# Local attention scores: one 128-key matmul, or two of 64 keys in 32x64 tiles of TensorE

## The chip, the cores and the metric

The kernel runs on one core of one Trainium2 chip. The core has five engines that run their own instruction streams and meet through semaphores: TensorE (PE in the profile; its weight loads are listed as PEld), VectorE (DVE), ScalarE (ACT), GpSimd (POOL) and SyncE (SP). TensorE multiplies a stationary operand, loaded first by a LDWEIGHTS instruction, with a moving operand that streams through, and writes sums to PSUM, which has eight banks of 2 KB on each of 128 partitions. A matmul that contracts over fewer than 128 rows, or gives fewer than 128 output partitions, occupies only a part of the array, a tile; "32x128" means 32 rows of contraction by 128 output partitions.

The metric is the device time of one execution in microseconds, the median of several runs. The profile is one execution, recorded instruction by instruction; its span runs from the first to the last instruction.

## What is computed

```python
# q_l, k_l, v_l: (8 batches, 8 heads, 512 tokens, 64); q_g, k_g, v_g: the same with 32 global tokens
s_g  = scale * q_g @ concat(k_g, k_l).T          # global queries see every key
out_g = softmax(s_g) @ concat(v_g, v_l)
s_ll = where(abs(pos_q - pos_k) <= 32, scale * q_l @ k_l.T, -1e9)   # local: a band of 65 keys
s_lg = scale * q_l @ k_g.T
out_l = softmax(concat(s_lg, s_ll)) @ concat(v_g, v_l)
x = concat(out_g, out_l, axis=2)                 # to (8 * 544 tokens, 512)
h = x @ w_in                                     # 512 -> 2048
out = (h / (1 + exp(-1.702 * h))) @ w_out        # 2048 -> 512
```

Inputs and outputs are float32; the products take bf16 operands and sum in float32.

## The kernel before

**Tiling of the attention.** The 64 pairs of batch and head are worked in 16 quads of four heads. In a quad, head j lies on the partitions 32j to 32j+31. A head has 64 features; 32 of them lie on the strip's partitions, and each 32-bit cell holds two bf16 features, so that a feature pair is picked by the index e (0 or 1) with a step of two elements. The tile `k` holds a quad's keys, `q` its queries, both turned by VectorE (L271, L275). Queries are stored as t, r (16 t by 32 r), and some rows of global queries are copied to the ends of the same tile (L285), so that one matmul gives the scores of a block of local queries and of the global queries.

**The scores, `S` (L300).** Keys are cut in four chunks c of 128. Two chunks make a round, so that a quad has two rounds. For chunk c only a window of queries can lie in the band: `WIN[c]` gives 10 or 12 values of r, and with 20 or 19 values of t these are 200 or 228 columns. For each chunk, `S` issues for e = 0 and 1, and for the four heads j, one matmul with lhsT = 32 rows by 128 keys and rhs = 32 rows by 200 or 228 columns (L314). It writes all 128 partitions of head j's bank, `ps[j]`: four heads, four banks. A call is thus a burst of 2 x 2 x 4 = 16 matmuls with their 16 weight loads. The first call of all is cut in two parts by query columns, since half of the queries are turned first.

**What follows a burst.** `X` (L347) applies the exponential on ScalarE, from the banks to the tile `e` in SBUF; `M` (L354) multiplies the band mask on VectorE. `gg` and `K` (L333) give the scores of the global keys in 32x32 tiles, `ekU` (L400) and `U` (L426) the products with values and the row sums, in 32x32 and 128x32 tiles; `Gm` (L444) those of the global queries.

**The feed-forward part.** `h_mm` (L495) multiplies x with `w_in`, 64 matmuls of 128x128 by 512 columns for a batch; `h_act` (L502, L503) applies the activation; `o_mm` (L520) multiplies with `w_out`, again 64 matmuls of 512 columns, in four groups of 16.

**The order of the work.** It is written out by hand: a Tile program whose scheduler is off (`manual_schedule`), so that each engine executes in the order of the Python code. In the steady part, `phase_o(i)` (L728) runs the output matmuls of batch i in four groups of 16, and puts the attention of batch i+1 between them: one call of `S` before each group, some of them followed by `gg`, `ekUs`, `U` and `Gm`. Then the 64 matmuls of `h_mm` for batch i+1 follow. DMAs for later batches are issued on GpSimd's queue (`load`, `load_v`), the outputs on SyncE's.

Of the kernel before, what the change touches and what calls it, by code (L numbers as in the profile page):

```python
# [20 lines left out]
def kernel(  # L21
# [12 lines left out]
    nc = tc.nc  # L34
# [211 lines left out]
    def bank(pair, j):  # L246
        return pair[j // 2][:, j % 2, :]

    class Quad:
# [50 lines left out]
        def S(self, rnd, split=False, added=False, part=None):  # L300
            if not added:
                self.bk[rnd] = self.spt(rnd)
            ps = self.bk[rnd] if split else [bank(self.bk[rnd], j) for j in range(4)]
            for c in (2 * rnd, 2 * rnd + 1):
                off = (0, 200, 0, 228)[c]
                r0, nr = WIN[c]
                t0, t1 = ((0, 20), (4, 23), (1, 20), (4, 24))[c]
                lo, hi = ((t0, t1) if part is None else (12, t1) if part else (t0, 12))
                off += (lo - t0) * nr
                n = (hi - lo) * nr  # L310
                for e in range(2):
                    for j in range(4):
                        p = slice(32 * j, 32 * j + 32)
                        nc.tensor.matmul(  # L314
                            ps[j][:, off : off + n],
                            lhsT=self.k[p, 128 * c : 128 * c + 128, e],
                            rhs=self.q[p, lo:hi, r0 : r0 + nr, e],
                            start=(e == 0 and not added), stop=(e == 1), skip_group_check=True,
                        )
            if not part:  # L320
                self.E[rnd] = att.tile([128, 4, RW + 32], BF16, name="e%d" % rnd)
            if split:
                self.gk(ps[2][:, RW : RW + 32], self.qg)
            self.ps = self.bk[rnd]
# [200 lines left out]
    def o_out(i, tci, op):  # L525
        ob = moe.tile([128, d_model], F32, name="ob", bufs=6)
        last = i == B and tci == B // 4 - 1
        for lo, hi in ((0, 320), (320, 512)) if last else ((0, 512),):
            if last:
                op = pbank("op")  # L530
                for fc in range(FC):
                    nc.tensor.matmul(op[:, lo:hi], lhsT=gTs[i][:, fc, tci * 128 : tci * 128 + 128],  # L532
                                     rhs=w_out_sb[:, fc, lo:hi], start=(fc == 0), stop=(fc == FC - 1))
            nc.scalar.activation(ob[:, lo:hi], op[:, lo:hi], AF.Copy, scale=0.5)  # L534
            for j in range(4):
                eng = nc.scalar if last and j % 2 else nc.sync
                if i < B:
                    rows = out[i * S + Sg : (i + 1) * S, :].rearrange("(r t) m -> t r m", t=16)[4 * tci + j]
                else:
                    r = (4 * tci + j) * S  # L540
                    rows = out[r : r + Sg, :]
                eng.dma_start(out=rows[:, lo:hi], in_=ob[32 * j : 32 * j + 32, lo:hi])  # L542
# [8 lines left out]
    a, c = Quad(0), Quad(1)  # L551
# [99 lines left out]
    a, c = nq[1]  # L651
# [48 lines left out]
    a, c = nq[2]  # L700
# [128 lines left out]
```

## Time and profile before

| | before |
|---|---|
| time, median of 3 runs | 307.6 us (307.58 to 308.48) |
| span of the profiled execution | 305.3 us |
| the profiled execution's own time | the page gives none apart from its span; the span is 2.3 us below the median |
| TensorE busy | 298.7 us, 98% |
| VectorE, ScalarE, GpSimd busy | 211.2, 169.3, 55.7 us |
| output matmuls, L520 | 528, 122.0 us busy |
| input matmuls of 512 columns, L495 | 496 (and 64 of 256 columns), 108.9 us busy |
| score matmuls, L314 | 528, 21.2 us busy, mean 280 ns each |
| weight loads of L314 | 528, mean 95 ns each |
| TensorE's granted clock | 1.000 |

How to read it. A matmul's duration is the time from its start until its results are in PSUM; matmuls are pipelined, so that a stream of 512-column matmuls that last 380 ns each starts one every 216 ns. Busy time counts overlapping matmuls once. The share of the chain that ended last tells what the end of the kernel waited for; idle time of an engine that is not in that chain costs nothing. In views of a short stretch, the number after x counts the instructions that touch the stretch, those that started before it among them.

### The profile page before, as it was taken

To read this page: it belongs to the slowest core of one execution; us is meant where nothing else is said; L and a number is where in the kernel's file an instruction comes from. 1 tells how busy PE (TensorE), PEld (TensorE's weight loads), DVE (VectorE), ACT (ScalarE), POOL (GpSimd) and SP (SyncE) were. 2 spreads that over 40 slices of the span, in tenths; PEclk is the share of its full clock that TensorE was granted. 3 is DMA by queue.
4 is the path that set the end of the run, shared out by engine and by line. 5 is a ranking of instruction groups with operands and counts; after the bars stand their busy time and mean duration, and the time that the engine had idled before them with its cause. 6 is when DMAs were issued, how large, how long until landed. Compare 5 with 4: busy or idle time off the path is not lost.

```text
span 305.3 us, 7862 instructions
## 1 busy us (share of the span) xinstructions
PE 298.7 (98%) x3265; PEld 148.5 (49%) x3265; DVE 211.2 (69%) x445; ACT 169.3 (55%) x282; POOL 55.7 (18%) x89
## 2 busy tenths in 40 slices
PE   7999999999999999999999999999999999999995
PEld 6454445445454455445454455445454454446653
DVE  6678858978868876777767876787677855573320
ACT  4738484585556655575457654665456661673421
POOL 8732755530050002300050002100000000000000
PEclk9999999999999999999999999999999999999999
DMA  7999999999399023941299024901130021101122
GB/s 191 178 206 207 197 180 230 211 170 131 82 112 191 10 56 84 151 97 37 54 122 170 4 56 89 101 0 48 44 86 2 2 66 48 46 0 36 36 63 75
DMA packets 56436, 29.52 MB, mean 97 GB/s; under 512 B 43088, under 2 KB 46288, under 8 KB 56400
## 3 DMA queue, kind: packets, MB, share of 16 engines
q0 software_dynamic: 46000, 16.98, 49.9%
q1 hardware_dynamic: 9920, 11.39, 14.3%
q10 hardware_dynamic: 480, 0.66, 0.7%
q8 instruction: 25, 0.41, 0.6%
q14 instruction: 11, 0.09, 0.1%
HBM read 35.13 MB, written 8.91 MB: 144 GB/s over the span
## 4 chain that ended last, share of the span: by engine, by line
PE 80%; DMA 15%; DVE 2%; POOL 1%; issue 1%; ACT 0%; ACTq 0%; DVEq 0%; POOLq 0%
PE op L520 34%; PE hp L495 33%; DMA rk<-in_k_l_dram 10%; PE s L314 5%; PE ov L426 4%; DMA rq<-in_q_l_dram 3%; DMA w_in_sb<-in_moe_w_in_dram 2%; PE ov L400 2%; DVE xL L459 1%; PE op L532 1%; PE s L444 1%; PE s L333 1%; ACTq L542 0%; ACT ob L534 0%; DVE e L354 0%
## 5 line engine op out<-in xcount | busy, mean ns | idle before, releaser
L520 PE MATMUL op<-w_out_sb,gT 128*128 128x512 bf16 x528 | 122.0, 380 | 0.0
L503 DVE SCALAR_TENSOR_TENSOR gT<-th,hp 128x512 bf16<-128x512 f32 (+1 forms) x140 | 91.2, 657 | 41.8 <-ACT th L502 40.7
L495 PE MATMUL hp<-xL,w_in_sb 128*128 128x512 bf16 x496 | 108.9, 379 | 0.3 <-DVE xL L459 0.2
L502 ACT ACTIVATE th<-hp 128x512 f32<-128x512 f32 (+1 forms) x140 | 79.9, 573 | 43.4 <-PE hp L495 39.9
L495 PEld LDWEIGHTS <-w_in_sb 128*128 128x128 bf16 x576 | 56.2, 98 | 64.7 <-issue 0.9
L520 PEld LDWEIGHTS <-gT 128*128 128x128 bf16 x528 | 49.2, 98 | 56.2 <-issue 3.5
L347 ACT ACTIVATE e<-s 128x856 bf16<-128x856 f32 x62 | 51.6, 884 | 12.1 <-PE s L444 7.0
L534 ACT ACTIVATE ob<-op 128x512 f32<-128x512 f32 (+2 forms) x35 | 20.5, 585 | 59.0 <-PE op L520 56.5
L89 POOL DMA_DIRECT2D v<-in_v_l_dram x24 | 18.7, 782 | 111.2 <-PE s L444 105.8
L450 DVE STREAM_TRANSPOSE sT<-ov 128x512 f32<-128x512 f32 x15 | 10.8, 717 | 26.9 <-PE ov L426 26.9
L354 DVE TENSOR_TENSOR e<-e,mask 128x1408 bf16<-128x1408 bf16 x28 | 24.4, 872 | 5.7 <-ACT e L347 5.7
L314 PE MATMUL s<-q,kT 32*128 32x228 bf16 (+5 forms) x528 | 21.2, 280 | 1.0 <-DVE q L275 1.0
L459 DVE TENSOR_TENSOR xL<-ov,rs 128x512 bf16<-128x512 f32 x30 | 19.3, 686 | 1.4
L314 PEld LDWEIGHTS <-kT 32*128 32x128 bf16 x528 | 10.9, 95 | 14.8 <-issue 6.6
L271 DVE STREAM_TRANSPOSE kT<-rk 128x512 f32<-128x512 f32 (+1 forms) x17 | 16.9, 994 | 1.0 <-DMA rk<-in_k_l_dram 1.0
L383 ACT ACTIVATE ek<-kb 128x512 bf16<-128x512 f32 x16 | 9.7, 608 | 9.2 <-PE kb L333 7.0
L426 PE MATMUL ov<-e,v 128*32 128x160 bf16 (+1 forms) x480 | 12.2, 239 | 0.0
L454 DVE STREAM_TRANSPOSE rs<-rT 128x512 f32<-128x512 f32 x16 | 11.4, 711 | 0.6
L275 DVE STREAM_TRANSPOSE q<-rq 128x512 f32<-128x512 f32 (+1 forms) x17 | 10.9, 641 | 1.0 <-ACT rq L558 1.0
L426 PEld LDWEIGHTS <-v 128*32 128x32 bf16 x512 | 10.0, 97 | 0.9 <-issue 0.9
L333 PE MATMUL kb<-q,kgT 32*32 32x512 bf16 x128 | 10.4, 387 | 0.0
L495 PE MATMUL hp<-xG,w_in_sb 128*128 128x256 bf16 x64 | 9.6, 273 | 0.0
(82 smaller groups left out, 170.6 us busy)
## 6 DMA issues: line engine op xcount, KB each, us to landing
out_dram<-ob SPq DMA_DIRECT2D x132, 64.0 KB, 1.7
v<-in_v_l_dram POOLq DMA_DIRECT2D x32, 128.0 KB, 6.0
rk<-in_k_l_dram POOLq DMA_DIRECT2D x6, 512.0 KB, 10.8
rq<-in_q_l_dram POOLq DMA_DIRECT2D x5, 512.0 KB, 8.6
w_out_sb<-in_moe_w_out_dram POOLq DMA_DIRECT2D x4, 512.0 KB, 10.8
rq<-in_q_l_dram POOLq DMA_DIRECT2D x5, 256.0 KB, 8.9
ek<-ek SPq DMA_DIRECT2D x13, 96.0 KB, 2.9
w_in_sb<-in_moe_w_in_dram POOLq DMA_DIRECT2D x4, 256.0 KB, 6.4
```

The lines of the kernel that those rows point to most:

```text
L89: nc.gpsimd.dma_start(out=vtiles[b % 2][p, s, :, :, :D], in_=vf[b, g][:, hs])
L271: nc.vector.transpose(self.kT.rearrange("p (r t) -> p t r", t=16)[:, lo:hi], loaded[self.b][0][:, self.u].bitcast(F32)[:, 32 * lo : 32 * hi])
L314: nc.tensor.matmul(ps[j][:, off : off + n], lhsT=self.k[p, 128 * c : 128 * c + 128, e], rhs=self.q[p, lo:hi, r0 : r0 + nr, e], start=(e == ...
L347: nc.scalar.activation(e[:, 2 * i : 2 * i + 2, :RW], self.ps[i][:, :, :RW], AF.Exp, scale=scale)
L354: nc.vector.tensor_mul(e, e, mask[:, rnd : rnd + 1, :].to_broadcast([128, 4, LW]))
L426: nc.tensor.matmul(ov[32 * j : 32 * j + 32, :].rearrange("p (t r) -> p t r", t=16)[:, :, r0 : r0 + nr], lhsT=lv, rhs=self.E[c // 2][:, j, ...
L459: nc.vector.tensor_mul(self.x[:, 2 * self.u + h, :], self.st[1 + h], self.st["rs"])
L495: nc.tensor.matmul(hp[:, : width(i)], lhsT=w_in_c[:, fc // 8, kc, fc % 8 // 2, :, fc % 2], rhs=(xL[i] if i < B else xG)[:, kc, :], start=( ...
L502: nc.scalar.activation(th[:, :n], hp[:, :n], AF.Tanh, scale=0.851)
L503: nc.vector.scalar_tensor_tensor(gTs[i][:, fc, :n], in0=th[:, :n], scalar=1.0, in1=hp[:, :n], op0=ALU.add, op1=ALU.mult)
L520: nc.tensor.matmul(op, lhsT=gTs[i][:, fc, tci * 128 : tci * 128 + 128], rhs=w_out_sb[:, fc, :], start=(first and fc == 4 * f4), stop=(fc = ...
L534: nc.scalar.activation(ob[:, lo:hi], op[:, lo:hi], AF.Copy, scale=0.5)
```

## The change

In the inner loop of `S`, each matmul of 128 keys becomes two of 64 keys: the stationary operand is cut in its columns (keys), and each half writes its 64 partitions of the same bank. The moving operand, the queries, is the same for both halves. The contraction is still over 32 rows, so that the tile of each matmul is 32x64. The order is chunk, e, head, half. Flags of accumulation, banks, columns and all that stands around the call stay.

```diff
                 for e in range(2):
                     for j in range(4):
                         p = slice(32 * j, 32 * j + 32)
-                        nc.tensor.matmul(
-                            ps[j][:, off : off + n],
-                            lhsT=self.k[p, 128 * c : 128 * c + 128, e],
-                            rhs=self.q[p, lo:hi, r0 : r0 + nr, e],
-                            start=(e == 0 and not added), stop=(e == 1), skip_group_check=True,
-                        )
+                        for h in (0, 64):
+                            nc.tensor.matmul(
+                                ps[j][h : h + 64, off : off + n],
+                                lhsT=self.k[p, 128 * c + h : 128 * c + h + 64, e],
+                                rhs=self.q[p, lo:hi, r0 : r0 + nr, e],
+                                start=(e == 0 and not added), stop=(e == 1), skip_group_check=True,
+                            )
```

## The prediction

> **What bounds the kernel now.** I read the page's shares first, then the chain that ended last, then the row of the changed line, and last the starts of single matmuls inside one burst of it.
>
> From the page of the kernel before: its span, the busy time of each engine, the chain by engine and by line, and two groups of section 5.
>
> ```profile
> span 305.3 us, 7862 instructions
> PE 298.7 (98%) x3265; PEld 148.5 (49%) x3265; DVE 211.2 (69%) x445; ACT 169.3 (55%) x282; POOL 55.7 (18%) x89
> ...
> PE 80%; DMA 15%; DVE 2%; POOL 1%; issue 1%; ACT 0%; ACTq 0%; DVEq 0%; POOLq 0%
> PE op L520 34%; PE hp L495 33%; DMA rk<-in_k_l_dram 10%; PE s L314 5%; PE ov L426 4%; DMA rq<-in_q_l_dram 3%; DMA w_in_sb<-in_moe_w_in_dram 2%; PE ov L400 2%; DVE xL L459 1%; PE op L532 1%; PE s L444 1%; PE s L333 1%; ACTq L542 0%; ACT ob L534 0%; DVE e L354 0%
> ...
> L314 PE MATMUL s<-q,kT 32*128 32x228 bf16 (+5 forms) x528 | 21.2, 280 | 1.0 <-DVE q L275 1.0
> ...
> L314 PEld LDWEIGHTS <-kT 32*128 32x128 bf16 x528 | 10.9, 95 | 14.8 <-issue 6.6
> ```
>
> TensorE is busy for 98% of the span, and L314, the line that changes, is 5% of the chain and idles 1.0 us before all its 528 matmuls. So whatever a burst of L314 gains or loses on TensorE, the end gains or loses; no other engine covers it. The chain in order of time shows one such burst between two runs of output matmuls.
>
> ```profile
> 129.95 7.55 PE hp L495 x35
> 137.50 0.60 PE s L314 x16
> 138.10 3.56 PE op L520 x16
> 141.66 0.59 PE s L314 x16
> ```
>
> Each piece begins where the last one stops: 16 score matmuls cost 0.59 to 0.60 us, with no slack on either side. Now the same burst cut into short stretches, instructions of L314 alone; the number after x counts the matmuls, then the weight loads, that touch the stretch.
>
> ```profile
> 137.43:137.45 0.02, 0.01 (x4) 0.02 (x5) 1.00 0.00 0
> 137.45:137.47 0.02, 0.02 (x4) 0.02 (x8) 1.00 0.00 0
> 137.47:137.56 0.09, 0.09 (x4) 0.08 (x8) 1.00 0.00 0
> 137.56:137.59 0.03, 0.03 (x8) 0.02 (x4) 1.00 0.00 0
> 137.59:137.69 0.10, 0.10 (x8) 0.09 (x4) 1.00 0.00 0
> 137.69:137.72 0.03, 0.03 (x12) 0.02 (x4) 1.00 0.00 0
> 137.72:137.81 0.09, 0.09 (x12) 0.09 (x4) 1.00 0.00 0
> 137.81:137.83 0.02, 0.02 (x12) 0.00 (x1) 1.00 0.00 0
> ```
>
> Four matmuls start together, one for each 32-row strip, then nothing starts for about 0.1 us, then the next four. By the single records the first matmuls of the four groups start at 137.437, 137.570, 137.700 and 137.814: pitches of 133 and 130 ns for the 228-column groups and 114 ns for the 200-column ones, at a granted clock of 1.00. Inside a group the starts lie 3 to 4 ns apart, 10 ns in all. The weight loads of the second group begin at 137.448, while the first group still runs: loads are hidden. For comparison, the value matmuls of L426, whose four tiles share all 128 rows and differ in their 32 columns:
>
> ```profile
> 142.80:142.82 0.02, 0.01 (x4) 1.00 0.00 0
> 142.82:142.88 0.06, 0.06 (x4) 1.00 0.00 0
> 142.88:142.90 0.02, 0.02 (x8) 1.00 0.00 0
> 142.90:142.96 0.06, 0.06 (x8) 1.00 0.00 0
> 142.96:142.99 0.03, 0.03 (x12) 1.00 0.00 0
> ```
>
> Here a group of 160 columns is followed after 80 ns (71 later on), one of 192 after 83. The plain 512-column matmuls of L520 follow each other every 216 ns, 0.42 ns a column; L426 is at 0.43 and a few ns on top, L314 at 114/200 = 0.57 and 133/228 = 0.58. So four row strips with all 128 columns pay about a third more per column than the stream itself needs.
>
> **The change part by part.** *Removed:* 528 matmuls 128 keys wide and their 528 weight loads. *Added:* 1056 of each, 64 keys wide, with the same columns of q. A group has eight tiles in place of four, a burst 32 pairs of load and matmul in place of 16. DVE, ACT, SP and POOL keep their instructions, order and waits; no DMA is added or moved. Number of bursts: 16 quads x 2 rounds = 32 (one is cut in two shorter halves, counted as one).
>
> (a) *Do the eight tiles of a group run side by side?* No row shows tiles that share a 32-row strip and split the columns. The nearest rows: L314 itself (four strips over the same columns, side by side) and L426 (four column strips over the same rows, side by side). Both dimensions of the split work alone, so I take side by side. Lower end: the groups fall to L426's price, N x 0.417 + 3 ns, 98 and 86 ns. Upper end: the halves take turns, twice 133 and 114.
>
> (b) *Pitch of a group.* It follows the stream: 0.556 N + 3.5 to 6 ns fits 70 ns (120 columns, in the first burst), 114 and 133. The third above 0.417 I expect to stay. L333 also uses four row strips, but each with its own 32 columns; its two groups of 512 follow at about 240 ns, 0.47 a column. What L314 has beyond it is four results for the same PSUM partition in four banks, and the change leaves that number alone. The 3.5 to 6 ns on top belong to four starts; with eight I take another 5. Three pitches lie inside a burst: +15 ns.
>
> (c) *The end of a burst.* What follows waits for the last start: with 12 ns between the first and last start of the last group, the next L520 comes 219 to 220 ns after the group's first start (137.44, 171.50); with 5 ns, 212 (181.63, 205.57). Eight starts at 3 to 4 ns make 25 instead of 10: +15 ns. Ends: +4, if the extra starts take 1 ns as the closest do, and +45, if they come as in the burst at 8.5 us, where four starts took 25 ns.
>
> (d) *Weight loads.* 64-column loads have no row. 128x128 loads mean 98 ns, 32x128 95, 128x32 97: the width shows nowhere, so I take no change. A group's loads start with the matmuls of the group before, more than 100 ns ahead; that cover ends if a load took over 114 ns.
>
> (e) *Issue.* 32 pairs per burst against 16. The tightest spacing where TensorE took a whole group is 20 matmuls of L444 in 144 ns, 7 ns a pair, against 114/8 = 14 needed. Taken as nothing, hidden by the 16 ns slots; the price without that cover is rival 2. The 1056 added instructions also lengthen the program's fetch from 0.41 MB (the instruction queue) by 1056/7862, 13%; TensorE's sequencer does not appear in the chain, so that is taken as nothing too.
>
> (f) *Changes of tile shape.* A burst is entered after 312 ns where a plain matmul has 216: 96 ns for the change of shape. The 32x64 shape stands where 32x128 stood, between the same neighbours, so the number of changes is equal: nothing.
>
> Sum: (15 + 15) ns x 32 = 0.96 us, taken as 1.0. On the profiled execution this is 305.3 to 306.3 of span. The page gives no time around its span; the median of the three runs, 307.6, lies 2.3 above it, and I add the same 2.3: 308.6 us.
>
> *A rule of the Trainium skill against the change, weighed.* "TensorE: Matmul & The Clock Gate", Part 3, The mechanism, says that a weight load overlaps a running matmul only where its row group differs. The trace does not agree: the second group's loads began at 137.448 on strips whose matmuls, started at 137.437 to 137.447, ran for another 0.1 us. By the rule each second half would wait for the first, and the sum would be rival 1's. *A second one:* "TensorEngine Tiling (Array Packing)", Restrictions, says that column tiling turns fast weight load off, and the first page (LDWEIGHTS) prices a load at its columns over 1.2 GHz, so 53 ns for 64. As an estimate from these pages, 27 ns more than a fast load (32 steps, 27 ns), seen once a burst if the first group can't hide it, gives 0.9 us and a time of 309.5. No run here shows a 64-column load.
>
> **Rivals.** *1. The halves take turns* (also what it would cost if the program still claimed a whole 32x128 tile for each half, so that the split does not do what it says). Each burst repeats its four pitches: 133 + 133 + 114 + 114 = 494 ns x 32 = 15.8 us, 323.4 us. For it: no row shows eight tiles. Against: L426's four tiles read the same 128 rows at the same time, each with a stream of its own.
>
> *2. The pairs don't come fast enough.* At 17.1 to 17.5 us, deep in a run of short matmuls, most starts lie 15 to 21 ns apart instead of in fours; 18 ns x 8 = 144 a group in place of 133 and 114: 2 x 11 + 2 x 30 = 82 ns, with (c) 97 ns x 32 = 3.1 us, 310.7 us; at 22 ns a pair (176 a group) it is 210 + 15 ns, 7.2 us, 314.8. Against: at that place the groups' pitches were still 82 and 71, so the spacing was not a limit, and before most bursts 16 or more long matmuls leave time to queue ahead.
>
> *3. Faster.* If the third on top comes from a stream that has to feed 128 columns, and not from the four results per partition, the halves go at L426's price: 2 x 98 + 2 x 86 = 368 against 494, less 126 ns, plus 15 at the end: 111 x 32 = 3.6 us less, 304.0 us. It decides once a group saves 11 ns: 44 - 15 = 29 ns a burst, 0.9 us. For it: L333 at 0.47 shows that four row strips alone do not cost 0.57. Against: L333 differs from L314 in the results per partition too, and those stay.
>
> **How the numbers follow.** About 0.3%, 0.9 us, is what a measurement of this kernel tells from no change. Forecast, groups side by side at nearly the old pitch: 0.61. Its own range is 307.7 (only (c) at +4 ns) to 309.8 ((b) at 3 x 8 and (c) at 45 ns); 1.0 is close to the bound, so 0.27 of it falls within 0.3% and 0.34 above. Rival 2 0.20, rival 1 0.10, rival 3 0.09. Faster 0.09, same 0.27, slower 0.34 + 0.20 + 0.10 = 0.64. The range leaves out rivals 1 and 3 (0.19): below, 307.0, a gain of 5 ns a group less the end's 4 ns (16 x 32 = 0.5 us); above, 314.0, nearly all of rival 2.
>
> **What the profile after would show.** The changed line with 1056 matmuls and a 32*64 tile; eight starts within about 25 ns, then a gap, and pitches of 135 to 140 and 117 to 122 ns; a burst in the chain at 0.62 to 0.63 us instead of 0.59 to 0.60; loads of about 97 ns; the rest unmoved. Rival 1 shows as bursts of 1.1 us with two sets of four starts per old pitch, rival 2 as evenly spaced starts, rival 3 as bursts under 0.58. The prediction is wrong if a pitch moves by more than 10 ns either way, or if the long matmuls after a burst start later than the last start explains.

## The result

The changed kernel takes 315.12 us (median of 4 runs, 313.82 to 317.22), the kernel before 307.59 (307.36 to 308.48): 2.5% slower, ratio 1.0251 with an interval of 1.0209 to 1.0292. The forecast was 308.6, with a range of 307.0 to 314.0. The span of the profiled execution grew from 305.3 to 313.2 us, by 7.9.

From the page of the changed kernel: span, busy times, chain by engine and by line, the changed line and its weight loads.

```profile
span 313.2 us, 8875 instructions
PE 297.3 (95%) x3750; PEld 150.6 (48%) x3793; DVE 210.5 (67%) x445; ACT 169.8 (54%) x282; POOL 55.6 (18%) x89
...
PE 92%; DMA 3%; issue 3%; ACT 0%; SPq 0%; DVE 0%; ACTq 0%
...
L315 PE MATMUL s<-q,kT 32*64 32x228 bf16 (+5 forms) x1056 | 22.4, 285 | 1.2 <-DVE q L275 1.2
...
L315 PEld LDWEIGHTS <-kT 32*64 32x64 bf16 x1056 | 13.0, 107 | 14.3 <-issue 7.8
```

The tile is 32x64, as asked, and the score matmuls are busy for only 1.2 us more than before. TensorE as a whole is not busier than before, 95% of a longer span (43 of its 3793 matmuls have no record in this profile, so that the 297.3 us are a little low), and "issue" has gone from 1% to 3% of the chain. So the loss is not in the work but in time when TensorE does nothing. TensorE's waits in the changed kernel (the line that waited, what ended the wait, us in total, times, longest) say where:

```profile
PE og L445 <- issue: 2.5, 1, 2.5
PE ov L427 <- issue: 2.2, 1, 2.2
PE s L334 <- DVE kgT L205: 1.9, 1, 1.9
...
PE s L315 <- DVE q L275: 1.2, 1, 1.2
```

Before, the list had none of the first three, and 1.0 us for the first queries. Two long waits have no semaphore behind them. The chain in order of time shows one of them, between two matmuls of one loop:

```profile
56.86 0.13 PE og L445 x16
56.99 2.50 issue
59.49 0.21 PE og L445 x4
```

The bursts themselves did about what was forecast. From the first matmul of a burst to the first that follows it, 30 bursts took 593.5 ns on the mean before and 629.3 ns now (the first call, cut in two, is left out). The 7.9 us add up: stops 2.23 + 2.50, the wait for the global keys 1.88, 0.28 more waiting for the first queries (1.24 against 0.96), and 30 x 36 ns = 1.07, together 7.96. Only the last term was in the forecast. (Other executions differ in the terms: the wait for the global keys and TensorE's clock, both taken up below, are not the same in each.)

**A first reading.** The program of TensorE is fetched in packets; the page's row for that queue is this one after the change (25 packets and 0.41 MB before):

```profile
q8 instruction: 29, 0.48, 0.6%
```

That is 16 KB a packet. With about 64 bytes an instruction (the 1056 added instructions made four more packets), a packet holds about 256 instructions, or 128 pairs of load and matmul. Weight loads counted before and inside the two stops of the changed kernel (the number after x):

```profile
0.00:19.60 19.60, 10.68 (x351) 1.00 1.27 178
19.60:21.78 2.18, 0.00 (x0) 1.00 0.98 137
21.78:57.00 35.22, 16.88 (x511) 1.00 1.46 198
57.00:59.48 2.48, 0.00 (x0) 1.00 1.20 245
```

The stops come after 351 and after 862 loads, 511 apart, four times 128 less one. By the records of the instruction queue, a packet started at 19.38 and landed at 20.33, and TensorE went on at 21.79; another started at 57.14, landed at 58.20, and TensorE went on at 59.49. In the kernel before, the 127 loads ahead of the first of these places, counted by instructions, took 6.55 us (15.51 to 22.05) and the packet had landed at 19.92; now they take 4.39 us (14.86 to 19.25). Theory: in stretches where short matmuls follow each other with no long ones between, called dense here, TensorE used up its instructions faster than the next 256 came. Rivals: chance; a cost of the 32x64 tile or its loads; a cost of the split in proportion to its bursts.

### The profile page after: what moved, and what is told of

It is laid out like the page before. It is cut to its first block, busy times and chain, and to the rows that moved or that the text cites. A ratio compares the mean times of both kernels' runs of the same rounds, so it can differ in the third digit from the quotient of the medians.

```text
span 313.2 us, 8875 instructions
## 1 busy us (share of the span) xinstructions
PE 297.3 (95%) x3750; PEld 150.6 (48%) x3793; DVE 210.5 (67%) x445; ACT 169.8 (54%) x282; POOL 55.6 (18%) x89
## 4 chain that ended last, share of the span: by engine, by line
PE 92%; DMA 3%; issue 3%; ACT 0%; SPq 0%; DVE 0%; ACTq 0%
PE op L521 37%; PE hp L496 36%; PE s L315 6%; PE ov L427 5%; DMA g32k<-in_k_g_dram 3%; PE ov L401 2%; PE s L496 1%; PE kb L334 1%; PE s L334 1%; PE op L533 1%; PE s L445 1%; PE s L297 0%; PE og L445 0%; PE s L427 0%; SPq L130 0%
## 5 line engine op out<-in xcount | busy, mean ns | idle before, releaser
L521 PE MATMUL op<-w_out_sb,gT 128*128 128x512 bf16 x497 | 119.6, 380 | 1.9 <-issue 0.5
L315 PE MATMUL s<-q,kT 32*64 32x228 bf16 (+5 forms) x1056 | 22.4, 285 | 1.2 <-DVE q L275 1.2
L315 PEld LDWEIGHTS <-kT 32*64 32x64 bf16 x1056 | 13.0, 107 | 14.3 <-issue 7.8
L384 ACT ACTIVATE ek<-kb 128x512 bf16<-128x512 f32 x16 | 9.6, 599 | 10.1 <-PE kb L334 8.0
L427 PEld LDWEIGHTS <-v 128*32 128x32 bf16 x512 | 10.1, 97 | 0.9 <-issue 0.9
L334 PE MATMUL kb<-q,kgT 32*32 32x512 bf16 x128 | 10.0, 387 | 0.0
L427 PE MATMUL ov<-e,ones 128*32 128x160 bf16 (+1 forms) x240 | 7.6, 242 | 2.2 <-issue 2.2
```

What stands on the lines that cost most here:

```text
L315: nc.tensor.matmul(ps[j][h : h + 64, off : off + n], lhsT=self.k[p, 128 * c + h : 128 * c + h + 64, e], rhs=self.q[p, lo:hi, r0 : r0 + nr, e],
L427: nc.tensor.matmul(ov[32 * j : 32 * j + 32, :].rearrange("p (t r) -> p t r", t=16)[:, :, r0 : r0 + nr], lhsT=lv, rhs=self.E[c // 2][:, j, ...
L521: nc.tensor.matmul(op, lhsT=gTs[i][:, fc, tci * 128 : tci * 128 + 128], rhs=w_out_sb[:, fc, :], start=(first and fc == 4 * f4), stop=(fc = ...
```

## The experiments

**1 and 2. Both kernels once more**, unchanged. The first:

> The changed kernel once more, to see which of the losses in its profile come back. Theory (instruction supply): TensorE runs out of fetched instructions in the two dense stretches of short matmuls; the idle stretches at 19.6 and 57.0 us, 2.2 and 2.5 us long and ended by no semaphore, come back within 1 us of the same place in the program, each with a fetch on the instruction queue that starts within 0.4 us of TensorE's last instruction. Rival (chance): they are elsewhere or gone, and the time falls by 2 us or more for each. The wait for the global keys at 9.4 to 12.0 us (2.2 us, ended by a DMA) I expect to differ between profiles. Time 314 to 317 us.

Measured: 315.19 us, ratio 1.022 (1.0171 to 1.027). In its profile, of the longest of the four executions (318.34 us), TensorE stops after 351 and after 862 loads, for 2.88 and 1.85 us, again with nothing that ends the wait. The fetches started 0.48 us after TensorE stopped and 0.55 us before, a little outside of the 0.4 us expected. The global keys were late again (a wait of 1.6 us at L334). The two stops are not chance.

> The kernel before once more, profiled on the same chip. Theory: no idle stretch of over 1 us on TensorE after 12 us; bursts of 0.59 to 0.60 us; global keys of the first two quads landed by 9 us. If the late landing is chance, it can show here too, and the time is then about 2 us longer than 307.6.

Measured: 307.24 us, no stop on TensorE after 12 us, global keys in use at 8.59 us. As theory expected.

**3 and 4. The split in a part of the quads.** Quads 0 to 3 hold the dense stretches before 60 us; quads 4 to 15 are worked between the long matmuls.

```diff
-                        for h in (0, 64):
-                            ... 64 keys
+                        w = 64 if self.Q >= 4 else 128      # run 4: 128 if self.Q >= 4 else 64
+                        for h in range(0, 128, w):
+                            ... w keys
```

> Only the quads from the fifth on are split (23 or 24 of the 32 calls). Theory (instruction supply in the dense stretches before 60 us): no stall there, the split costs only its bursts, 24 x 35 ns = 0.8 us: 308.4 us. Rival (the loss belongs to the split itself, in proportion): 24/32 of 7.5 us, 313.2 us.

Measured: 308.22 us, ratio 1.0049 (1.0016 to 1.0082). TensorE's waits have no "issue" left. The bursts, in the chain:

```profile
172.09 0.63 PE s L316 x24
172.72 3.56 PE op L522 x16
176.28 0.63 PE s L316 x26
```

0.63 us against 0.59 to 0.60 before; by the records 627.2 ns on the mean of 24, so 24 x 33.7 ns = 0.8 us; the medians differ by 0.66. Three quarters of the split carry a tenth of the loss by the medians, a fifth by the ratio.

> Only the first four quads are split (8 of the 32 calls, 288 added instructions). Theory (instruction supply): both stalls are there, 2.2 + 2.5 us, plus 8 x 35 ns and what the late global keys cost in that run: 312 to 315 us. Rival (in proportion): 8/32 of 7.5 us, 309.5 us.

Measured: 314.06 us, ratio 1.0207 (1.0177 to 1.0237). Eight calls carry 6.5 of the 7.5 us, the lower clock of the last section included. Weight loads before and in its idle stretches:

```profile
0.00:13.60 13.60, 7.18 (x224) 1.00 1.27 184
13.60:14.70 1.10, 0.00 (x0) 1.00 1.26 205
0.00:19.10 19.10, 9.72 (x351) 1.00 1.25 191
19.10:20.70 1.60, 0.00 (x0) 1.00 1.13 209
0.00:58.10 58.10, 27.11 (x862) 0.97 1.41 197
58.10:59.20 1.10, 0.00 (x0) 1.00 1.11 251
```

The stops of the changed kernel are there, and a third one after load 224, one packet (127 pairs) ahead of load 351. Here VectorE took up the global keys early (8.46 us, 11.42 in the changed kernel). In the changed kernel TensorE stood waiting for them at 10.1 to 12.0 us, which gave the fetch its time. So it is in all six profiles of kernels with stops, those of the runs below included: where the keys were late (the changed kernel, runs 1 and 5) there is no stop after load 224, where they were early (runs 4, 6 and 9) there is. One stop takes the place of the other.

**5. Instructions without the split.** Tiles stay 32x128; the first four quads get as many extra pairs as the split adds there.

```diff
+                    def extra():
+                        for j in range(4):
+                            p = slice(32 * j, 32 * j + 32)
+                            nc.tensor.matmul(ps[j][:, off : off + 2], lhsT=warm[p, 0:128],
+                                             rhs=warm[p, 0:2], start=False, stop=False, ...)
+                    if e == 1 and self.Q < 4:
+                        extra()
                     for j in range(4):
                         ... the score matmul of 128 keys, as before
+                    if e == 0 and self.Q < 4:
+                        extra()
```

> No split at all. In the first four quads each call gets 16 extra pairs of weight load and matmul in the old 32x128 tile (144 pairs in nine parts of calls, as many as the split adds there; zeros added to two columns), after the first and before the second four of a chunk. Theory (instruction supply): what counts is how many instructions stand in the dense stretches, so TensorE stops without a semaphore at the same instruction numbers as with the split, near the 351st and the 862nd weight load: 310 to 315 us. Rival (the 32x64 tile or its loads cause the stops): no stop, only the extra pairs' own time, 8 x 16 x 5 to 10 ns = 0.6 to 1.3 us: 308.2 to 308.9 us.

Measured: 314.24 us, ratio 1.0182 (1.0101 to 1.0262). Loads before and in the stops:

```profile
0.00:20.50 20.50, 11.16 (x351) 0.92 1.25 180
20.50:21.50 1.00, 0.00 (x0) 1.00 1.08 178
21.60:57.40 35.80, 17.29 (x511) 1.00 1.48 194
57.40:60.40 3.00, 0.00 (x0) 0.96 1.15 236
```

The same places to the load, without a single 32x64 tile. The number of instructions is enough to make the stops; the shape of the tile is not needed.

**6 and 7. Less traffic during the second dense stretch, first try.** Two loads were moved down the program text, in the changed kernel and in the one before:

```diff
-    load_v(2)
-    load(3)
     ...
+    load_v(2)
+    load(3)
     load_v(3)
     load(4)
```

> The changed kernel with the loads of the values of batch 2 and of q and k of batch 3 issued after the second dense stretch, behind the weights of the global part, so that fewer bytes are moving at 50 to 58 us. Theory (the fetch is late because the DMA engines are full): the fetch that was requested around 52.5 us starts within 2 us, not 4.6, the stop near the 862nd load shrinks to below 1 us or goes, the one near the 351st stays: 1.5 to 3 us less than the changed kernel, 312 to 313.5 us. Rival (the fetch starts late whatever else moves): the stop stays at 2 to 2.7 us and the time at 315.

> The same move of two loads in the kernel before, as the control of the run above: both theories expect no change, 307.3 to 308 us, since nothing waits for these loads before 90 us.

Measured: 315.08 us (ratio 1.0214, 1.0145 to 1.0283) and 307.56 (0.9992, 0.9951 to 1.0032). The edit did not do what was meant: between the old place and the new one nothing else is issued on GpSimd's queue, and no wait, so that the loads went out at 44 to 49 us all the same. The run says nothing on the traffic. As one more profile of the changed kernel it shows stops after 224, 351 and 862 loads of 1.98, 1.69 and 1.41 us, with the global keys in use at 8.69 us: again the early keys and the third stop together.

**8. The halves in another order**, heads inside halves, from the fifth quad on.

```diff
-                    for j in range(4):
-                        for h in range(0, 128, w):
+                    for h in range(0, 128, w):
+                        for j in range(4):
```

> Split from the fifth quad on, with all four heads of the lower half first and then the four of the upper, so that neighbours in the order differ in their 32-row strip. For the burst alone: if the 35 ns a burst come from a second start on the same strip, the bursts fall to 0.60 to 0.61 us; if from the number of starts and the 64-column load in the first group, they stay at 0.62 to 0.64 us. Time within 0.5 us of the run with the late split, 308.2 us.

Measured: 308.15 us; 632.8 ns a burst on the mean of 24, against 627.2 in run 3. The bursts did not fall, so the cost is not a second start on the same strip. What is left is the eight starts or the 64-column loads; no run separates these two.

**9 and 10. The loads behind a wait.** Now the two loads stand behind the load of the values of batch 3, which waits for the second dense stretch to end.

```diff
     load_v(3)
+    load_v(2)
+    load(3)
     load(4)
```

> The changed kernel with the loads of the values of batch 2 and of q and k of batch 3 put behind the load of the values of batch 3 on GpSimd's queue; that load waits for the end of the second dense stretch, so these bytes can move only after it (in the run with the loads moved before, the queue had passed them at 44 to 49 us all the same). Theory (the fetch comes late where the DMA engines are full): less than 150 GB/s at 52 to 58 us, the stop near the 862nd weight load below 0.7 us or gone, 1.5 to 3 us less than the changed kernel: 312 to 313.5 us. Rival (late whatever moves): the stop stays at 1.4 to 3 us, 315 us.

Measured: 313.42 us, ratio 1.0182 (1.0151 to 1.0213), 1.7 us less than the changed kernel by the medians. The time alone does not settle it, since this interval overlaps those of the changed kernel (1.0209 to 1.0292, and 1.0171 to 1.027 in run 1); the trace does. DMA traffic and TensorE's busy time around the second dense stretch, here:

```profile
52.00:54.00 2.00, 1.88 (x82) 1.00 0.34 92
54.00:56.00 2.00, 2.00 (x36) 1.00 0.43 107
56.00:58.00 2.00, 2.00 (x89) 1.00 0.13 33
58.00:60.00 2.00, 2.00 (x27) 1.00 0.28 72
```

and in the changed kernel:

```profile
52.00:54.00 2.00, 1.95 (x72) 1.00 1.88 207
54.00:56.00 2.00, 2.00 (x37) 1.00 2.16 194
56.00:58.00 2.00, 0.99 (x64) 1.00 1.53 237
58.00:60.00 2.00, 0.35 (x5) 1.00 1.13 238
```

The last number of a line is GB/s. With 33 to 107 GB/s in place of 194 to 238, the packet that started at 57.14 in the changed kernel started at 54.39, that is 0.80 us after TensorE had begun the packet ahead in place of 4.66, and the stop after load 862 is gone, though the 127 loads ahead of it take the same 4.29 us. The stops after 224 and 351 loads stay (2.49 and 0.62 us), where nothing was moved. The second is short because the packet ahead of it lasted long, 5.1 us; TensorE's clock was at half for 3.41 us of that.

> The same order of loads in the kernel before, the control. Both theories: no stop was there, so 307.3 to 308.0 us; up to 2 us slower if the loads of batch 2 or 3 now come late.

Measured: 307.33 us, ratio 1.0001 (0.9985 to 1.0017): the order of loads by itself is worth nothing.

**11. Denser still, but late.** Run 3 with 32 extra pairs in each split call (eight 32x64 matmuls of zeros over two columns after the first and before the second group of a chunk), 64 pairs a call.

```diff
+                    if e == 1 and self.Q >= 4:
+                        extra()          # 4 heads x 2 halves, 2 columns of zeros
                     ... the split score matmuls
+                    if e == 0 and self.Q >= 4:
+                        extra()
```

> Split from the fifth quad on, and there 32 extra pairs of zeros over two columns in each call (64 pairs a call, twice the density that the split gives). After 80 us the DMA engines are mostly idle. Theory (it takes dense instructions and full DMA engines together): no idle stretch of TensorE over 0.5 us after 80 us, only the extra pairs' own time, 24 x 0.12 to 0.24 us on 308.2: 311 to 314 us. Rival (density alone makes the stop): a stop of over 1 us in most of the 12 stretches from a call to the end of its value matmuls, 320 us or more.

Measured: 313.16 us. All waits on TensorE are before 60 us, none of them on "issue", and a stretch of 20 us with the denser calls in it has no gap:

```profile
140.00:160.00 20.00, 20.00 (x508) 1.00 0.21 50
```

The calls are dense enough for the test. In one of the shortest stretches of a packet's length the weight loads are (the number after x counts those that touch the stretch)

```profile
214.91:218.70 3.79, 2.31 (x135) 1.00 0.19 45
```

so that 128 of them take 3.79 us, less than the 4.3 to 4.4 ahead of the stops of the changed kernel. So density alone does not stop TensorE where some 50 GB/s move. By the records a call takes 811.9 ns in place of the 627.2 of run 3: the extra pairs cost 24 x 0.18 = 4.4 of the 4.9 us over run 3, and this profile has 1.4 us of waiting for the global keys, which run 3 has not.

## Why the prediction was wrong

**The step that failed is (e), Issue.** It took two things as nothing. The first, the rate at which pairs start inside a group, was right: starts inside a split group lie 0 to 17 ns apart and the later pitches are the old ones. The second was wrong: the longer program was priced by its total, 13% more, and found hidden because TensorE's sequencer was not in the chain. (Against TensorE's own instructions, which that queue brings, it was 16%, from 25 packets to 29; the 7862 of the sum count all engines.) What counts is one packet of 256 instructions against the time in which the next one arrives. Runs 3, 4, 5, 9 and 11 put two conditions on a stop: short matmuls follow each other for a whole packet (127 loads in 4.0 to 4.5 us at full clock where the kernel before took 6.55), and the DMA engines move some 200 GB/s, so that the packet starts late. In the 14 stops of the six profiles that have them, the packet starts 3.3 to 5.0 us after TensorE has begun the packet ahead, and TensorE goes on 1.3 to 1.5 us after it has landed. An absent wait in the profile before was read as ample slack. It was little: the second packet landed at 19.92 and the 352nd load ran at 22.06; the changed kernel took 1.46 us from landing to use (20.33 to 21.79), so that 0.7 us were to spare, and the split takes 2.2 us from the packet ahead. That makes 1.5 of the stop's 2.23 us; the rest is a later start of the packet, 4.16 us after TensorE had begun the packet ahead where it was 3.47 before. The start at 18.98 us and the landing at 19.92 stood in the trace of the kernel before.

**Steps (b), (c) and (d): right in sum, not in place.** 30 ns a burst were forecast, 36 measured. (b) put 5 ns on each of three pitches; in the burst at 144.86 they are 148, 130 and 114 ns against 133, 130 and 114, so the first group carries it all. On the mean of 30 bursts the first pitch grew by 15 ns (124.5 to 139.5) and the other two by 0.8 each, which is also the prediction's own sign of being wrong, a pitch that moves by more than 10 ns. (c) forecast 25 ns from the first to the last start; the first groups have 23 to 24, the last 10 to 39, and the time from the last group's first start to what follows grew by 19 ns (223 to 242), not 15. (d) took the load as unchanged; it went from 95 to 107 ns on the mean.

**Step (a): right.** Eight tiles run side by side. Eight matmuls of a burst start within 24 ns, then nothing for 0.1 us (the number after x counts score matmuls that touch the stretch):

```profile
144.86:144.89 0.03, 0.03 (x8) 1.00 0.00 0
144.89:144.99 0.10, 0.10 (x8) 1.00 0.00 0
144.99:145.03 0.04, 0.04 (x15) 1.00 0.00 0
145.03:145.12 0.09, 0.09 (x16) 1.00 0.00 0
```

*Rival 1* (the halves take turns, 323.4 us) is refuted by these lines, and with it what the rule on row groups would have made of a burst. *Rival 2* (pairs come too slowly, 310.7) was near in kind: TensorE does lack instructions. But it expected evenly spaced starts in all 32 calls; the lack shows as whole stops, two or three in a profile, and none that begins after 60 us. *Rival 3* (faster) is refuted: the later pitches are the old ones, so the third above 0.417 ns a column stays with 64-column tiles. *(f)* held: a burst is entered 309 to 310 ns after a 512-column matmul's start, where it was 311 to 312. (The lower end of the forecast's range comes out at 307.1 us from its own terms, not 307.0; nothing rests on it.)

The estimate from "TensorEngine Tiling (Array Packing)" and "TensorE: Matmul & The Clock Gate", 27 ns a burst for a load without the fast mode, has the sign and the place right: the first pitch grew by some 15 ns and the loads by 12, though no run shows that the slower load is what lengthens the pitch. (The page gives the 32 steps of the fast load as theory for fp8; the operands here are bf16.) It was not the loss.

"Runtime: NRT & Kernel Launch", Instruction fetch mechanics, says that the instruction memory is refilled in blocks of 16 KiB, 256 instructions, and that crossing a block's end costs little, mostly hidden. The runs agree on the blocks (16 KB packets, stops 127 and 511 loads apart). They do not agree on the cost where both conditions hold: 0.6 to 3.05 us a stop.

**What stays open.** Why a packet is asked for or starts so late under traffic was not taken apart; only that it does, and that less traffic cures it. The stops at 13 to 22 us were not cured, since the loads of the weights that run there can't be left out; that they have the same cause is argued from run 5, their places and the times of their packets, not shown by a run with less traffic. Why the first global keys come into use at 8.5 to 9.4 us in most runs and at 10.3 to 11.6 in others was not found; a wait for them shows in runs 8 (1.0 us) and 11 (1.4 us) too, where the early calls are as in the kernel before, so that the 1.88 us of the first profile are not shown to be the split's.

## What to carry to other kernels

Count instructions by the packet, not by the program: where 256 TensorE instructions in a row are short, and large loads are in flight, ask how many us they last and when the next packet lands before splitting a matmul in two. A stop on "issue" with no semaphore, at fixed distances in instruction numbers, is the sign of it; the test is to add as many empty instructions without the change. An edit that doubles instructions for no fewer columns is best kept out of such stretches: the same split cost 0.5% (ratio) outside of them, in 24 calls, and 2.1% inside, in eight.

## What was not expected of the hardware

Around the stops the array's clock can fall. In run 5 the stretch after the stop of 3.05 us had a granted clock of 0.57:

```profile
60.00:64.00 4.00, 3.25 (x12) 0.57 1.38 207
```

The fall is the same wherever the profiles show it ahead of the kernel's end: a clock of 0.50 for 3.41 us. In run 9, after the stop that ended at 16.34 us, it is

```profile
17.71:21.12 3.41, 3.41 (x98) 0.50 1.13 210
```

In run 4 it begins at 21.68, after a stop of 1.7 us that ended at 20.74. In the changed kernel's own profile the clock stayed at 1.00 through stops of 2.2 and 2.5 us. The mean clock listed with an execution was 0.995 or less in 19 of the 26 executions of kernels with stops, and in 8 of 73 of the others (the kernel before, and runs 2, 3, 7, 8, 10 and 11). So the fall goes with the stops, but it comes without them too. In run 5 seven 512-column matmuls took from 61.00 to 63.78 us, 2.78 us where 7 x 216 ns would be 1.51. As an estimate from the 0.50 and the 3.41 us, a fall costs up to 1.7 us; so the price of a stop is not only its length.
